# Clamp and square of the first block's activation: from two GpSimd instructions to one VectorE instruction

## The chip, the cores and the metric

The kernel runs on one core of one Trainium2 chip. The metric is device time in microseconds: 1082.85 us is the median of three runs of the kernel before (1081.09 to 1083.65). A core has five queues that run in order and wait for each other by semaphores: TensorE (PE, matrix products into PSUM), VectorE (DVE), ScalarE (ACT), GpSimd (POOL) and SyncE (SP, which issues most transfers).

## The reference

Three parts follow each other. Attention with a soft cap on 4 batches of 12 heads, 448 positions and 64 channels; a feed-forward layer with 768 x 2048 and 2048 x 768 weights; a mixture of 8 experts, each token going to one of them. The change concerns the activation of the feed-forward layer:

```
h = x @ w_in
g = h                      where h >= 1
g = 0                      where h <= -1
g = (h + 1)**2 / 4         between
return g @ w_out
```

The weights w_in and w_out come as 64-bit floats; the kernel takes them as pairs of 32-bit words and converts them itself.

## The kernel before

The 1792 tokens are worked in four blocks b of 448, one for each batch. A block has its attention (six pairs of heads, `attn_gen`), its feed-forward layer (`gemm1` and `gemm2`, together `moe1_gen`) and its routing to the experts (`route_gen`). The feed-forward layer of block b runs woven with the attention of block b + 1. Block 0 is special: beside it the weights are converted from 64 bits (`conv_one`: one ScalarE instruction that writes cv or cvs, three VectorE instructions L1022, L1024 and L1027 on raw or raws, and two transfers for each of 40 pieces, 16 of w_in and 24 of w_out).

`gemm1` makes 16 tiles h (f = 0 to 15) of 128 x 448 in PSUM. All products are made with each operand split in two parts, a rounded one (hi: wh, xh, gh) and its remainder (lo: wl, xl, gl); so each h takes 18 matmuls (L1320 to L1322), nine for each half of its weights. Weights are loaded as wr, rounded to wh by ScalarE (L1289) and their remainder wl made by VectorE (L966). The PSUM tag "m" has two buffers, so h(f + 2) can begin only when h(f) has been read for the last time.

The activation works on a tile g in SBUF. With t = min(relu((h + 1)/2), 1) it is max(h, t * t). In code (`gemm1`): ScalarE makes the relu (L1327); in block 0 (`G_POOL = (0,)`) GpSimd then clamps (L1329) and squares (L1330), while in the blocks 1 to 3 one VectorE instruction does both (L1332); VectorE takes the maximum with h (L1333, the last reading of the PSUM buffer); then ScalarE rounds to gh (L1334) and VectorE makes gl (L966). GpSimd also copies the last keys into a block-diagonal tile kd (L1099) and scales the attention's output x (L1168).

The order on each queue is not that of the code. Every step is declared with `op(engine, cost, ...)`, and `Plan.run` simulates the engines with these costs, in nanoseconds, and issues the steps in the order in which they would become ready; where two are ready, the earlier declared one goes first, shifted by `URGENCY` of its tile. So an engine, a cost or a number of steps that is changed at one place can move others. The costs that matter here are `gs(448)` = 710 for the clamp, `g_(448)` = 1090 for the square and `d1(448)` = 531 for a VectorE instruction. From the last part on (the experts) the order is written out by hand.

Of the kernel before, what the change touches and what calls it, by code (L numbers as in the profile page):

```python
# [15 lines left out]
ALU = mybir.AluOpType  # L16
# [5 lines left out]
B, H, S, D = 4, 12, 448, 64  # L22
# [17 lines left out]
PACE = 65000  # L40

URGENCY = {'h': 30, 'slot': 38, 'ev': -60, 'kq': -15, 'gh': 60, 't': 16, 'w': -8, 'yr': -15, 'sc': 8, 'rt': 16, 'yt': 15, 'lt': -38, 'lp': 60, 'pt': 15, 'ph': -22, 'kd': 45, 'xh': -45, 'g': -60, 'den': 22, 'pick': -60, 'vn': 60, 'fill': -60}
G_POOL = (0,)


def constants():
# [645 lines left out]
class Plan:  # L692
# [13 lines left out]
    def op(self, eng, cost, fn, rd=(), wr=(), dma=0, more=(), duty=1.0, lazy=None):  # L706

        s = Step()
        s.eng, s.cost, s.fn, s.dma, s.more, s.duty = eng, cost, fn, dma, more, duty
        s.lazy = self.BACKLOG if lazy is None else lazy  # L710
        s.users, s.gates = [], []
        s.name = str(getattr(wr[0][0], "name", wr[0]))
        s.rank = (len(self.steps) + URGENCY.get(re.search("[a-z]+", s.name)[0], 0), len(self.steps))
        deps = set()
        syms = set()
        rd = list(rd) + [(x[0].gate, 0) for x in (*rd, *wr) if isinstance(x[0], Sym) and x[0].gate]
        for k in rd:
            if k in self.last:
                deps.add(self.last[k])
            self.reads.setdefault(k, []).append(s)  # L720
        for k in wr:
            if k in self.last:
                deps.add(self.last[k])
            deps.update(self.reads.pop(k, ()))
            self.last[k] = s
        for k in (*rd, *wr):
            if isinstance(k[0], Sym):
                syms.add(k[0])
                if k[0].within:
                    syms.add(k[0].within[0])  # L730
        deps.discard(s)
        s.deps = len(deps)
        for d in deps:
            d.users.append(s)
        s.syms = sorted(syms, key=lambda x: x.name)
        for x in s.syms:
            if x.left == 0:
                self.order.setdefault((x.tag, x.name if x.tag is None else None), []).append(x)
            x.left += 1
        s.ready = 0.0  # L740
        self.steps.append(s)
# [166 lines left out]
def kernel(ctx, tc, q, k, v, cap, w_in, w_out, w_gate, w1, w2, consts, cols, out):  # L908

    nc = tc.nc  # L910
    PE, ACT, DVE, POOL, SP = nc.tensor, nc.scalar, nc.vector, nc.gpsimd, nc.sync
# [37 lines left out]
    op = P.op  # L949
# [7 lines left out]
    d1 = lambda n: 1.04 * n + 65  # L957
    d2 = lambda n: 0.52 * n + 70
    g_ = lambda n: 2.3 * n + 60
    gs = lambda n: 1.45 * n + 60  # L960
    mm = lambda n, N=S: n * N / 2.37
    KDC = 210
    SPQ, PQ = 560, 1040
# [1 line left out]
    def sub_lo(eng, out, a, hi):  # L965
        eng.tensor_sub(out, a, hi.bitcast(F32))  # L966
# [283 lines left out]
    def split_x(b):  # L1250
        for i in range(NDC):
            x = xs[b, i]
            op("ACT", a_(S), lambda x=x, i=i: ACT.copy(xh[b].t[:, i], x.t), rd=[(x, 0), (x, 1)], wr=[(xh[b], i)])
            op("DVE", d1(S), lambda x=x, i=i: sub_lo(DVE, xl[b].t[:, i], x.t, xh[b].t[:, i]),
               rd=[(x, 0), (x, 1), (xh[b], i)], wr=[(xl[b], i)])
# [5 lines left out]
    def unit_load(u):  # L1261
        b, i = divmod(u, NU)
        if b >= B:
            return
        n = 384 if i < 2 * NFC else 512
        while b == 0 and words and conv_n[0] <= (i // 2 if i < 2 * NFC else i - NFC):
            conv_one(conv_n[0])
        r = Sym(MP, [128, 512], F32, "wr", 3, f"wr{u}")
        if words:
            src = wi_s[i] if i < 2 * NFC else wo_s[i - 2 * NFC]  # L1270
            go = lambda: SP.dma_start(r.t[:, :n], src)
        else:
            if i < 2 * NFC:
                f, hf = divmod(i, 2)
                src = w_in[hf * 384 : hf * 384 + 384, f * 128 : f * 128 + 128]
            else:
                d, g = divmod(i - 2 * NFC, 4)
                src = w_out[g * 512 : g * 512 + 512, d * 128 : d * 128 + 128]
            go = lambda: SP.dma_start(r.t[:, :n].rearrange("p (a f) -> p a f", f=128), src.rearrange("(a p) f -> p a f", p=128))
        op("SP", SPQ, go, rd=[("w", i)], wr=[(r, 0)], dma=n * 512)  # L1280
        wraw[u] = r, n

    def unit_split(u):
        if u >= B * NU:
            return
        r, n = wraw.pop(u)
        hi = Sym(MP, [128, 512], F32R, "wh", 4, f"wh{u}")
        lo = Sym(MP, [128, 512], F32R, "wl", 4, f"wl{u}")
        op("ACT", a_(n), lambda: ACT.copy(hi.t[:, :n], r.t[:, :n]), rd=[(r, 0)], wr=[(hi, 0)])  # L1289
        op("DVE", d1(n), lambda: sub_lo(DVE, lo.t[:, :n], r.t[:, :n], hi.t[:, :n]), rd=[(r, 0), (hi, 0)], wr=[(lo, 0)])  # L1290
        wsp[u] = hi, lo

    def step(u):
        unit_load(u + 4)
        unit_split(u + 2)
# [3 lines left out]
    def gemm1(b):  # L1299
        u = b * NU  # L1300
        if b == 0:
            for i in range(4):
                unit_load(i)
            unit_split(0)
            unit_split(1)
        split_x(b)
        for f in range(NFC):
            if b == B - 1 and f % 2:
                pm = Sym(PSE, [128, 512], F32, "y", 2, f"h{b}_{f}")
            else:  # L1310
                pm = Sym(PM, [128, 512], F32, "m", 2, f"h{b}_{f}")
            for hf in range(2):
                step(u)
                hi, lo = wsp.pop(u)
                u += 1

                def go(hi=hi, lo=lo, hf=hf, pm=pm):
                    for a in range(3):
                        i = 3 * hf + a
                        PE.matmul(pm.t[:, :S], part_of(hi, a), xh[b].t[:, i], start=i == 0, stop=False)  # L1320
                        PE.matmul(pm.t[:, :S], part_of(hi, a), xl[b].t[:, i], start=False, stop=False)  # L1321
                        PE.matmul(pm.t[:, :S], part_of(lo, a), xh[b].t[:, i], start=False, stop=i == NDC - 1)  # L1322

                op("PE", mm(9), go, rd=[(hi, 0), (lo, 0)] + [(x[b], 3 * hf + a) for x in (xh, xl) for a in range(3)], wr=[(pm, 0)])
                yield 1701
            t = Sym(XP, [128, S], F32, "g", 2, f"g{b}_{f}")
            op("ACT", 520, lambda t=t, pm=pm: ACT.activation(t.t, pm.t[:, :S], AF.Relu, bias=half, scale=0.5), rd=[(pm, 0), ("half", 0)], wr=[(t, 0)])  # L1327
            if b in G_POOL:
                op("POOL", gs(S), lambda t=t: POOL.tensor_scalar(out=t.t, in0=t.t, scalar1=1.0, scalar2=None, op0=ALU.min), wr=[(t, 0)])  # L1329
                op("POOL", g_(S), lambda t=t: POOL.tensor_mul(t.t, t.t, t.t), wr=[(t, 0)])  # L1330
            else:
                op("DVE", d1(S), lambda t=t: DVE.scalar_tensor_tensor(out=t.t, in0=t.t, scalar=1.0, in1=t.t, op0=ALU.min, op1=ALU.mult), wr=[(t, 0)])  # L1332
            op("DVE", d1(S), lambda t=t, pm=pm: DVE.tensor_max(t.t, pm.t[:, :S], t.t), rd=[(pm, 0)], wr=[(t, 0)])  # L1333
            op("ACT", a_(S), lambda t=t, f=f: ACT.copy(gh[b].t[:, f], t.t), rd=[(t, 0)], wr=[(gh[b], f)])  # L1334
            op("DVE", d1(S), lambda t=t, f=f: sub_lo(DVE, gl[b].t[:, f], t.t, gh[b].t[:, f]), rd=[(t, 0), (gh[b], f)], wr=[(gl[b], f)])
# [29 lines left out]
    def moe1_gen(b):  # L1365
        yield from gemm1(b)
        yield from gemm2(b)
# [157 lines left out]
    b = B - 1  # L1525
    P.gate("opened", lambda: opened(0), (AP, PA))
    weave((gemm1(b), 56000), (chosen(), 50000))

    def swap():
# [81 lines left out]
    with tc.manual_schedule(engines=set(engines)):  # L1611
        b = B - 1
# [64 lines left out]
```

## Time and profile before

| | |
|---|---|
| runs of the kernel before | 1083.65, 1081.09, 1082.85 us |
| profiled execution | 1089.11 us, its span 1087.3 us |
| TensorE busy (matmul) | 1020.2 us, 94% of the span |
| VectorE busy | 527.8 us, 49% |
| ScalarE busy | 527.7 us, 49% |
| GpSimd busy | 176.7 us, 16% |
| mean granted TensorE clock | 0.977 of full speed |

A row of the profile gives an engine, a line of the code, the tile written and the tiles read. "Busy" counts an instruction from its start to its end; a TensorE that waits for an operand or for a free PSUM buffer is idle, and the profile names what ended that idle time. The granted clock is told as a share of full speed (2.4 GHz); 0.50 is the lower of the two levels, 1.2 GHz.

### The profile page before, as it was taken

The page shows a single profiled execution, that of the slowest core. Times are in us where ns is not written, and L with a number is a line of the kernel's source. Part 1 is how long each engine was busy: PE and PEld are TensorE (multiplying, and loading weights), DVE is VectorE, ACT ScalarE, POOL GpSimd, SP SyncE. Part 2 cuts the span into 40 slices and gives each one's busy share as a digit, 9 for nine tenths or more (in the row PEclk, how much of TensorE's full clock was granted, in tenths as well). Part 3 has the DMA queues.
Part 4 walks back from the last instruction along what each step waited for, and adds up shares of the span by engine and source line. Part 5 has one row for each costly group of instructions (what it writes and reads, how often), then busy time and mean ns, then how long its engine had stood idle before and what let it go on. Part 6 is the DMA issues. An engine that isn't in the chain of part 4 may idle for free. (4 is left out here: it accounts for less than half of the span.)

```text
span 1087.3 us, 17434 instructions
## 1 busy us (share of the span) xinstructions
PE 1020.2 (94%) x5546; PEld 784.8 (72%) x5546; DVE 527.8 (49%) x1038; ACT 527.7 (49%) x872; POOL 176.7 (16%) x231
## 2 busy tenths in 40 slices
PE   5887799899999999999999999999999999999995
PEld 2434676678776776966776789889767768889994
DVE  5786799776556653356664237663460101111110
ACT  4876577564656755376666345463332212222221
POOL 1123465310031100011001001100311111111110
PEclk9998899999999999999999999999999999999998
DMA  7777877879454444344443335683128884211111
GB/s 212 222 208 214 252 215 222 254 220 286 141 100 121 111 115 107 107 114 99 109 115 88 97 96 120 206 270 105 41 59 310 309 296 164 61 47 46 45 45 34
DMA packets 167810, 162.57 MB, mean 150 GB/s; under 512 B 90805, under 2 KB 139437, under 8 KB 167682
## 3 DMA queue, kind: packets, MB, share of 16 engines
q1 hardware_dynamic: 164274, 148.06, 46.8%
q0 software_dynamic: 3408, 13.00, 3.6%
q8 instruction: 56, 0.92, 0.3%
q14 instruction: 72, 0.59, 0.2%
HBM read 190.39 MB, written 24.39 MB: 198 GB/s over the span
## 5 line engine op out<-in xcount | busy, mean ns | idle before, releaser
L966 DVE TENSOR_TENSOR wl<-wr,wh 128x384 fp32r<-128x384 f32 (+1 forms) x224 | 143.1, 640 | 134.1 <-ACT wh L1289 133.3
L1289 ACT CAST wh<-wr 128x384 fp32r<-128x384 f32 (+1 forms) x224 | 124.2, 556 | 126.5 <-PE y L1353 69.9
L1320 PE MATMUL h<-xh,wh 128*128 128x448 f32 x384 | 150.0, 391 | 12.1 <-DVE g L1333 11.7
L1322 PE MATMUL h<-xh,wl 128*128 128x448 f32 x384 | 144.0, 375 | 2.0 <-DVE wl L966 2.0
L1352 PE MATMUL y<-gh,wh 128*128 128x448 f32 x384 | 144.0, 375 | 0.4 <-DVE g L1333 0.4
L1321 PE MATMUL h<-xl,wh 128*128 128x448 f32 x384 | 144.2, 376 | 0.0
L1354 PE MATMUL y<-gh,wl 128*128 128x448 f32 x384 | 140.8, 367 | 0.9 <-DVE wl L966 0.9
L1353 PE MATMUL y<-gl,wh 128*128 128x448 f32 x384 | 140.5, 366 | 0.0
L1320 PEld LDWEIGHTS h<-xh,wh 128*128 128x128 f32 x384 | 74.6, 194 | 49.5 <-issue 23.2
L1135 PE MATMUL pv<-t,vn 128*64 128x448 f32 x384 | 96.9, 587 | 11.0 <-ACT t L1115 3.8
L1114 ACT ACTIVATE t<-sc,csc 128x896 f32<-128x896 f32 x96 | 87.2, 914 | 25.1 <-PE sc L1105 15.0
L500 DVE TENSOR_TENSOR hl<-ht,hh 128x512 fp32r<-128x512 f32 x26 | 18.0, 691 | 164.9 <-ACTq L599 159.9
L1115 ACT ACTIVATE t<-t,capx 128x896 f32<-128x896 f32 x96 | 91.0, 951 | 2.1
L1352 PEld LDWEIGHTS y<-gh,wh 128*128 128x128 f32 x384 | 72.1, 188 | 22.4 <-issue 15.3
L1322 PEld LDWEIGHTS h<-xh,wl 128*128 128x128 f32 x384 | 74.7, 195 | 9.1 <-DVE wl L966 2.4
L1321 PEld LDWEIGHTS h<-xl,wh 128*128 128x128 f32 x384 | 74.8, 195 | 5.9 <-DVE xl L966 0.2
L1354 PEld LDWEIGHTS y<-gh,wl 128*128 128x128 f32 x384 | 72.1, 188 | 7.9 <-DVE wl L966 1.9
L512 PE MATMUL ey<-w2h,hh 128*128 128x384 f32 x208 | 75.3, 362 | 2.7 <-issue 2.7
L1353 PEld LDWEIGHTS y<-gl,wh 128*128 128x128 f32 x384 | 72.2, 188 | 5.5
L514 PE MATMUL ey<-w2h,hl 128*128 128x384 f32 x208 | 70.6, 339 | 0.0
L513 PE MATMUL ey<-w2l,hh 128*128 128x384 f32 x208 | 70.5, 339 | 0.0
L480 PE MATMUL ph<-w1h,ex 128*128 128x512 f32 x156 | 64.3, 412 | 2.1 <-issue 2.1
(254 smaller groups left out, 1637.7 us busy)
## 6 DMA issues: line engine op xcount, KB each, us to landing
s<-in_moe_w_dram SPq DMA_DIRECT2D x84, 512.0 KB
s<-in_moe_w_dram SPq DMA_DIRECT2D x104, 384.0 KB
wr<-wi_s SPq DMA_DIRECT2D x128, 192.0 KB
wr<-wo_s SPq DMA_DIRECT2D x96, 256.0 KB
raws<-in_moe_w_in_dram SPq DMA_DIRECT2D x12, 768.0 KB
raw<-in_moe_w_out_dram SPq DMA_DIRECT2D x12, 512.0 KB
wo_s<-cv SPq DMA_DIRECT2D x24, 256.0 KB
kq<-in_k_dram SPq DMA_DIRECT2D x48, 112.0 KB
```

Source lines behind the costliest of these rows:

```text
L512: nc.tensor.matmul(o, hh[:, i], self.w2h[f][:, c], start=f == 0, stop=False)
L966: eng.tensor_sub(out, a, hi.bitcast(F32))
L1114: op("ACT", a_(n * S) + 35, lambda: ACT.activation(t.t[:, :n], pt.t[:, :n, :S], AF.Tanh, scale=csc), rd=[(pt, 0), ("cap", 0)], wr=all_)
L1115: op("ACT", a_(n * S) + 85, lambda: ACT.activation(t.t[:, :n], t.t[:, :n], AF.Exp, scale=capx), wr=all_)
L1135: PE.matmul(pvs.t[rows(j), :S], s["vn"][:, c, j], px(j), start=c == 0, stop=c == 3)
L1289: op("ACT", a_(n), lambda: ACT.copy(hi.t[:, :n], r.t[:, :n]), rd=[(r, 0)], wr=[(hi, 0)])
L1320: PE.matmul(pm.t[:, :S], part_of(hi, a), xh[b].t[:, i], start=i == 0, stop=False)
L1321: PE.matmul(pm.t[:, :S], part_of(hi, a), xl[b].t[:, i], start=False, stop=False)
L1322: PE.matmul(pm.t[:, :S], part_of(lo, a), xh[b].t[:, i], start=False, stop=i == NDC - 1)
L1352: PE.matmul(pm.t[:, :S], part_of(hi, f % 4), gh[b].t[:, f], start=f == 0, stop=False)
L1353: PE.matmul(pm.t[:, :S], part_of(hi, f % 4), gl[b].t[:, f], start=False, stop=False)
L1354: PE.matmul(pm.t[:, :S], part_of(lo, f % 4), gh[b].t[:, f], start=False, stop=f == NFC - 1)
```

## The change

In block 0 the clamp and the square become the VectorE instruction of the other blocks: (t min 1) * t. The constant `G_POOL` and the cost `gs` go. The lines behind them move up by two to six.

```diff
-G_POOL = (0,)
...
-    gs = lambda n: 1.45 * n + 60
...
-            if b in G_POOL:
-                op("POOL", gs(S), lambda t=t: POOL.tensor_scalar(out=t.t, in0=t.t, scalar1=1.0, scalar2=None, op0=ALU.min), wr=[(t, 0)])
-                op("POOL", g_(S), lambda t=t: POOL.tensor_mul(t.t, t.t, t.t), wr=[(t, 0)])
-            else:
-                op("DVE", d1(S), lambda t=t: DVE.scalar_tensor_tensor(out=t.t, in0=t.t, scalar=1.0, in1=t.t, op0=ALU.min, op1=ALU.mult), wr=[(t, 0)])
+            op("DVE", d1(S), lambda t=t: DVE.scalar_tensor_tensor(out=t.t, in0=t.t, scalar=1.0, in1=t.t, op0=ALU.min, op1=ALU.mult), wr=[(t, 0)])
```

Since the planner sees other engines and costs, the order of other steps moves too. GpSimd loses the 32 instructions, VectorE gains 16; of some 5500 TensorE rows about 50 stand elsewhere, nearly all in blocks 0 and 1. Three places matter.

VectorE around the first two activations, before. The names carry the pair's or tile's number f and a serial number; wl is a weight remainder, raws and cvs belong to the conversion, kl is a remainder of the keys:

```order
L1027 SCALAR_TENSOR_TENSOR cvs<-cvs,raws 128x768
L966 TENSOR_TENSOR wl_1178<-wr_1096,wh_1174 128x384
L1333 TENSOR_TENSOR g_0_1172<-h_0_968,g_0_1172 128x448
L1022 TENSOR_SCALAR raws<-raws 128x768
L966 TENSOR_TENSOR wl_1217<-wr_1142,wh_1201 128x384
L1024 SCALAR_TENSOR_TENSOR raws<-raws 128x768
L966 TENSOR_TENSOR kl_1228<-pt_0_1184,kh_1215 128x448
L1333 TENSOR_TENSOR g_1_1199<-h_1_1012,g_1_1199 128x448
```

And VectorE at the same place now:

```order
L1025 SCALAR_TENSOR_TENSOR cvs<-cvs,raws 128x768
L1326 SCALAR_TENSOR_TENSOR g_0_1172<-g_0_1172 128x448
L964 TENSOR_TENSOR wl_1178<-wr_1096,wh_1174 128x384
L1327 TENSOR_TENSOR g_0_1172<-h_0_968,g_0_1172 128x448
L1020 TENSOR_SCALAR raws<-raws 128x768
L1326 SCALAR_TENSOR_TENSOR g_1_1201<-g_1_1201 128x448
L1022 SCALAR_TENSOR_TENSOR raws<-raws 128x768
L1327 TENSOR_TENSOR g_1_1201<-h_1_1012,g_1_1201 128x448
```

The new instruction (now L1326) stands two places ahead of the maximum (now L1327), with a wl or a conversion between; kl has moved to a later place.

TensorE between h3 and h4, before (sc are attention scores, pt transposed keys or queries, pv and su the products with values and ones):

```order
L1322 MATMUL h_3_1247<-xh_624,wl_1217 128x448
L1080 MATMUL pt_1_1290<-ct,kq_1106 128x112 x4
L1105 MATMUL sc_3_1296<-qh_1043,kd 128x448 x2
L1105 MATMUL sc_3_1296<-ql_1061,kd 128x448
L1135 MATMUL pv_1123<-t_2_1219,vn_98 64x448 x2
L1135 MATMUL pv_1123<-t_3_1312,vn_98 64x448 x2
L1139 MATMUL su_1337<-ta_1134,one 32x448
L1139 MATMUL su_1337<-t_3_1312,one 32x448
L1139 MATMUL su_1337<-ta_1134,one 32x448
L1139 MATMUL su_1337<-t_3_1312,one 32x448
L1320 MATMUL h_4_1356<-xh_624,wh_1241 128x448
```

TensorE between h3 and h4 now:

```order
L1320 MATMUL h_3_1228<-xh_624,wl_1238 128x448
L1106 MATMUL sc_2_1274<-qh_1043,kh_1004 128x448 x2
L1106 MATMUL sc_2_1274<-qh_1043,kl_1010 128x448 x2
L1106 MATMUL sc_2_1274<-ql_1061,kh_1004 128x448 x2
L1078 MATMUL pt_1_1292<-ct,kq_1106 128x112 x4
L1318 MATMUL h_4_1317<-xh_624,wh_1223 128x448
```

The group sc_2, which stood in front of h2, has come here; sc_3 now follows h4, one pv follows h5, and the other pv and su follow h6. On ScalarE the relus of g2 and g3 stood behind a tanh of sc_3; they now stand behind the tanh of sc_2 and one wh.

VectorE for the activations of h2 and h3, before (rt are sums of the attention, qh rounded queries):

```order
L966 TENSOR_TENSOR wl_1326<-wr_1265,wh_1306 128x384
L1024 SCALAR_TENSOR_TENSOR raw_1189<-raw_1189 128x768
L1162 TENSOR_TENSOR rt_1288<-rt_1288 32x2x14
L1085 CAST qh_1344<-pt_1_1290 128x448
L1027 SCALAR_TENSOR_TENSOR cv_1271<-cv_1271,raw_1189 128x768
L1333 TENSOR_TENSOR g_2_1320<-h_2_1205,g_2_1320 128x448
L1163 RECIPROCAL rt_1288<-rt_1288 32x2x14
L1333 TENSOR_TENSOR g_3_1323<-h_3_1247,g_3_1323 128x448
```

And VectorE for the same activations now:

```order
L964 TENSOR_TENSOR wl_1300<-wr_1250,wh_1290 128x384
L1326 SCALAR_TENSOR_TENSOR g_2_1298<-g_2_1298 128x448
L1326 SCALAR_TENSOR_TENSOR g_3_1302<-g_3_1302 128x448
L1327 TENSOR_TENSOR g_2_1298<-h_2_1191,g_2_1298 128x448
L1327 TENSOR_TENSOR g_3_1302<-h_3_1228,g_3_1302 128x448
L1025 SCALAR_TENSOR_TENSOR cv_1265<-cv_1265,raw_1189 128x768
L964 TENSOR_TENSOR gl_1288<-g_2_1298,gh_1245 128x448
L964 TENSOR_TENSOR gl_1288<-g_3_1302,gh_1245 128x448
L964 TENSOR_TENSOR wl_1338<-wr_1263,wh_1307 128x384
L1160 TENSOR_TENSOR rt_1271<-rt_1271 32x2x14
L964 TENSOR_TENSOR kl_1350<-pt_0_1184,kh_1207 128x448
```

Four activation instructions now stand together, and kl, from which GpSimd makes the copies kd that sc_3 reads, stands behind them.

## Rows read from the trace of the kernel before

**Rows 1.** Windows of all engines: stretch, then busy us (instructions); PEclk, DMA share, GB/s

```profile
100.00:210.00 110.00, 94.60 (x453) 70.12 (x449) 91.61 (x138) 67.83 (x111) 56.09 (x50) 0.93 0.79 235
210.00:300.00 90.00, 89.12 (x471) 66.56 (x469) 59.18 (x106) 54.36 (x90) 7.84 (x15) 1.00 0.74 226
```

**Rows 2.** Waits of TensorE, 95 to 215 us: us in total, times, longest

```profile
PE h L1320 <- DVE g L1333: 11.7, 6, 4.7
```

**Rows 3.** Groups by line, GpSimd, 100 to 212 us: busy us, mean ns | idle before

```profile
L1329 POOL TENSOR_SCALAR g<-g 128x448 f32<-128x448 f32 x16 | 26.4, 1650 | 42.4 <-ACT g L1327 42.3
L1330 POOL TENSOR_TENSOR g<-g 128x448 f32<-128x448 f32 x16 | 16.8, 1052 | 1.0
```

**Rows 4.** Groups by line and shape, ScalarE, 100 to 212 us

```profile
L1289 ACT CAST wh<-wr 128x384 fp32r<-128x384 f32 x26 | 13.1, 505 | 4.7 <-PE h L1321 2.6 <-PE h L1322 1.2 <-DMA wr<-wi_s 0.9
...
L1114 ACT ACTIVATE t<-sc,csc 128x896 f32<-128x896 f32 x10 | 10.1, 1009 | 0.9 <-PE sc L1108 0.8
L1327 ACT ACTIVATE g<-h,half 128x448 f32<-128x448 f32 x16 | 10.0, 630 | 3.8 <-PE h L1322 3.8
```

**Rows 5.** Groups by line and shape, VectorE, 100 to 212 us

```profile
L966 DVE TENSOR_TENSOR wl<-wr,wh 128x384 fp32r<-128x384 f32 x26 | 18.2, 700 | 2.8 <-ACT wh L1289 2.8
...
L1027 DVE SCALAR_TENSOR_TENSOR cv<-cv,raw 128x512 int32<-128x512 int32 x11 | 10.2, 931 | 0.0
L1333 DVE TENSOR_TENSOR g<-h,g 128x448 f32<-128x448 f32 x16 | 9.8, 616 | 8.2 <-POOL g L1330 8.2
L1024 DVE SCALAR_TENSOR_TENSOR raw<-raw 128x512 int32<-128x512 int32 x11 | 9.6, 876 | 0.3
```

**Rows 6.** The same, VectorE, 212 to 330 us

```profile
L966 DVE TENSOR_TENSOR wl<-wr,wh 128x384 fp32r<-128x384 f32 x16 | 8.9, 555 | 10.5 <-ACT wh L1289 10.5
...
L1024 DVE SCALAR_TENSOR_TENSOR xraws_xh<-xraws_xh 128x512 int32<-128x512 int32 x6 | 4.2, 692 | 0.1
L1027 DVE SCALAR_TENSOR_TENSOR cv<-cv,xraws_xh 128x512 int32<-128x512 int32 x6 | 4.1, 690 | 0.1
...
L1332 DVE SCALAR_TENSOR_TENSOR g<-g 128x448 f32<-128x448 f32 x6 | 3.7, 622 | 7.1 <-ACT g L1327 7.1
L1333 DVE TENSOR_TENSOR g<-h,g 128x448 f32<-128x448 f32 x6 | 3.7, 617 | 0.0
```

**Rows 7.** Timeline of all engines around h2: start us, us, engine, line [idle before]

```profile
105.16 1.37 DVE L1024 SCALAR_TENSOR_TENSOR raws<-raws 128x768 int32<-128x768 int32 x1
...
105.93 0.47 PE L1108 MATMUL sc<-qh,kh 64*128 64x448 f32 x2
...
107.44 1.28 DVE L966 TENSOR_TENSOR wl<-wr,wh 128x384 fp32r<-128x384 f32 x1
...
108.65 0.61 DVE L1333 TENSOR_TENSOR g<-h,g 128x448 f32<-128x448 f32 x1
...
109.31 0.52 PE L1320 MATMUL h<-xh,wh 128*128 128x448 f32 x1 [2.52 <-DVE g L1333]
```

**Rows 8.** Windows of 1 us, TensorE: busy us (instructions), PEclk, DMA share, GB/s

```profile
112.00:113.00 1.00, 1.00 (x5) 0.50 1.06 358
...
133.00:134.00 1.00, 1.00 (x5) 0.75 0.73 171
```

**Rows 9.** Timeline of TensorE around h4

```profile
118.59 0.65 PE L1105 MATMUL sc<-qh,kd 128*128 128x448 f32 x2
...
121.77 0.97 PE L1135 MATMUL pv<-t,vn 128*64 128x448 f32 x4 [1.43 <-ACT t L1115]
...
128.31 0.74 PE L1320 MATMUL h<-xh,wh 128*128 128x448 f32 x1 [4.67 <-DVE g L1333]
```

**Rows 10.** Timeline of GpSimd around h4

```profile
119.58 2.89 POOL L1099 CAST kd<-kh 64x64 fp32r<-64x64 f32 x2 [6.54 <-PE sc L1105]
...
126.66 1.82 POOL L1330 TENSOR_TENSOR g<-g 128x448 f32<-128x448 f32 x2
```

**Rows 11.** Timeline of TensorE near the end of the first product

```profile
201.18 0.47 PE L1320 MATMUL h<-xh,wh 128*128 128x448 f32 x1 [2.67 <-DVE g L1333]
```

## The prediction

> **What bounds the kernel now.** I began with the windows by stage. Behind 210 us TensorE is the bound: it is busy 89.12 of 90 us at full clock [rows 1], so whatever is saved ahead of 210 us can reach the end, and nothing behind it waits for the instructions that the diff touches. The first block's first product lies in 100 to 210 us. There TensorE is busy only 94.60 of 110 us and its mean granted clock is 0.93, while VectorE is busy 91.61 and GpSimd 56.09 us [rows 1].
>
> Then I read who holds TensorE there: 11.7 us in 6 waits for L1333, the maximum that frees the PSUM buffer of an h [rows 2]. Two such buffers exist, so h2 cannot begin before the maximum on h0. Last, the chain that leads to L1333. Today it is relu 0.63 us (ScalarE), clamp 1.65 and square 1.05 (GpSimd), maximum 0.62 (VectorE): 3.95 us without queueing [rows 3 to 5].
>
> **What is removed and added.** GpSimd loses 16 clamps and 16 squares: 26.4 + 16.8 = 43.2 us [rows 3]. Nothing else gains from its free time, since GpSimd is nowhere the bound. VectorE gains 16 of the L1332 form that blocks 1 to 3 already run, at 0.622 us each [rows 6]. Back to back, an instruction begins a little before its predecessor ends (wl began at 107.44 and lasted 1.28, the next began at 108.65: 0.07 us [rows 7]; I reckon with 0.09), so the load is about 16 x 0.53 = 8.5 us.
>
> What VectorE gets back: in 100 to 212 us several of its forms are longer than behind it. The weight remainder wl takes 0.700 against 0.555 us (26 of them: 3.8 us), cv 0.931 against 0.690 (11: 2.7), raw 0.876 against 0.692 (11: 2.0) [rows 5, 6]. That is 8.5 us. The maximum, with one operand in PSUM, is not longer (0.616 against 0.617). GpSimd's busy time is the difference of the two stretches, and 43.2 of its 56.09 us go, so I credit three quarters: 6.5 us. The bounds are 0 (another cause) and 8.5. VectorE's load then changes by 8.5 - 6.5 = +2 us, between 0 and +8.5; its 8.2 us of waiting for GpSimd [rows 5] cover that.
>
> The Trainium skill (SBUF — State Buffer, section "SBUF: two separate sides") says that GpSimd shares a port pair with VectorE, exclusively and for a whole instruction, when the VectorE instruction has two SBUF inputs. The longer wl and the unchanged maximum [rows 5, 6] agree with it; that the mean grows by only 0.15 us, far less than a clamp lasts, shows that most instructions meet no GpSimd one. The rule also speaks against the change: the new instruction has two SBUF inputs and can be held by what GpSimd keeps, the kd and x work, 56.09 - 43.2 = 12.9 of 110 us [rows 1, 3]. At one hit in seven and 0.7 us each this would be 16 x 0.14 x 0.7 = 1.6 us by the rule (an estimate), and the sum below would be 4 instead of 5.5 us.
>
> The chain becomes relu 0.63, new instruction 0.62, mostly one wl of 0.55 that the planner puts between, and maximum 0.62: 2.4 us against 3.95, so 1.5 us shorter [rows 4 to 6]. What that is worth I read at three places.
>
> **Place A, h2.** TensorE stops at 106.79 and begins h2 at 109.31 [rows 7]. In the new order the VectorE queue is raws (begins 105.16, now unstretched, next after 0.87), cvs (0.87), the new instruction (0.53), wl (0.47), maximum: it begins at about 107.9, not 108.65. So h2 begins 0.75 us earlier. But the planner, which reckons on an earlier buffer, has moved the group sc_2 behind h3; those 0.86 us (105.93 to 106.79) were work inside the wait. Net -0.1 us: nothing. The clock, at 0.50 after this wait [rows 8], drops as before.
>
> **Place B, h4.** Here the trace has its longest wait. Work resumes with pt and sc_3 (118.59) and TensorE then waits 1.43 and 4.67 us until h4 begins at 128.31 [rows 9]. GpSimd first does four kd casts, 119.58 to about 124.0, and ends the two squares at 128.48 [rows 10]. Now, with h3 done at about 118.3 - 0.75 = 117.5: sc_2 to 118.4 and its latency, tanh 1.0 (from 118.8), wh 0.5, two relus (pitch 0.53, the second ends at 121.3), new instruction on g3 to 121.9, maximum on g2 to 122.5, h4 at about 122.6. That is 5.7 us earlier. Not yet done then are sc_3, the two pv and su: 128.31 - 4.67 - 118.59 - 1.43 = 3.6 us of work that today stands inside the wait. Net +2.1 us. Bounds: -3.6 if h4 still begins at 128.3, and +5.7 if all the deferred work finds a later wait to hide in. The clock ran at half from 128.31 until late in 133 to 134 [rows 8], costing about 2.6 us; the new wait of some 4 us (with pt inside) is still longer than the one at A, so I take it that the clock drops again, for the shorter time seen at A, and credit 0.8 (bounds 0 and 2.6).
>
> **Place C, h6 to h15.** Of the 11.7 us, 11.7 - 2.52 - 4.67 - 2.67 = 1.8 us are three short waits [rows 2, 7, 9, 11], each under 0.9; a chain 1.5 us shorter removes them. The wait of 2.67 before 201.18 [rows 11] shrinks by 1.5, and the dip of the clock behind it with it (about 1.7 us by the same kind of reckoning; I take half, 0.9). Sum +4.2; bounds 0 and 6.2.
>
> **New waits.** At B the cast kl moves from ahead of the first maxima to behind gl of g3, and sc_3 needs GpSimd's copies of it; VectorE reaches kl near 126 and h4 covers TensorE until about 127.7, so 0 to 1 us is late there. Other moved groups (one sc, one pv between h and y; in block 1 a few rows around its route) have no wait today that I can price. I charge 1.5 us for all, with bounds 0 and 6.
>
> **Sum.** -0.1 + 2.1 + 0.8 + 4.2 - 1.5 = 5.5 us. The profiled execution took 1089.11 us (its span of 1087.3 and 1.8 around it), so it would take 1083.6. The median of the three runs is 1082.85, 6.3 below the profiled one; the waits are those of an order that is the same in both, so I subtract the same 5.5 us: **1077.3 us**.
>
> **Rivals.**
> 1. The gain is whole: all 11.7 us of waits go and about 3 of the dips, 14.7 us, giving 1068. For it: VectorE's load hardly grows. Against it: the reordering uses up places A and B in part, and relu on g2 now stands behind the tanh of a group that itself waits for h3.
> 2. It is given back to the transfers: the DMA share is 0.79 in this stretch and 0.74 in the next [rows 1], and 1.06 in single microseconds [rows 8]. The w_out conversions follow on the heels of their use; if data cannot come earlier, the y product waits and the time stays at about 1082.5. Against it: 5.5 us fewer over 200 us lift the share by 3% only.
> 3. Slower, at place B: the filler of 3.6 us was moved away from the wait, but the wait stays, because tanh, wh, two relus and four VectorE instructions stand in series after h3, and any one late (a weight transfer, a conversion in front) moves h4. It decides at h4 later than 128.31 - 3.6 = 124.7; I reckon 122.6, a margin of 2.1 us. At today's 128.3 the price is 3.6 us: 1086.5.
> That the change does not do what it says is excluded by the new order: no such GpSimd instruction is left, and 16 VectorE ones stand in.
>
> **How the numbers follow.** Forecast 53%, rival 1 15%, rival 2 15%, rival 3 17%. A measurement of this kernel tells about 0.2% (2.2 us) from no change. The forecast's own range, 1073 to 1080, is on the faster side, as is rival 1: faster 68%. Rival 2 is no change, 15%, and rival 3 slower, 17%. The range reaches down to 1068, the full gain, and up to 1085, where a good half of rival 3 lies above.
>
> **What would show it.** In 95 to 215 us the waits for the maximum should fall from 11.7 to about 5 us, nearly all of it at A and B; VectorE's busy time there should stay within 90 to 95 us although 16 instructions more run, with wl at 0.56 to 0.60 us; h4 should begin 5 to 6 us earlier; block 1 should begin earlier by the whole gain. I am wrong if wl stays at 0.70, if h4 begins later than 124.7, or if waits for VectorE's wl, kl or ql take the place of those for the maximum.

## The result, and the profile after

The changed kernel takes 1068.26 us (1066.93 to 1072.70, four runs) against 1082.88 us of the kernel before in the same session: ratio 0.9868, 95% interval 0.9830 to 0.9906. Run once more in a later session (e9 below) it stood at 0.9896 (0.9858 to 0.9934). I use the mean of the two, 0.9882 +- 0.0027, or 12.8 us of 1085, when it is compared with experiments of other sessions. The direction was forecast and the size was not: 5.5 us forecast, 14.6 us in the first comparison and 12.8 us over both.

The profiled execution of the changed kernel took 1066.93 us (span 1065.1, granted clock 0.985). These windows of all engines answer to [rows 1]:

```profile
100.00:210.00 110.00, 104.41 (x531) 78.65 (x530) 93.76 (x164) 76.18 (x122) 16.96 (x22) 0.98 0.87 269
210.00:300.00 90.00, 88.06 (x466) 65.59 (x465) 62.27 (x121) 55.39 (x94) 7.00 (x12) 0.98 0.65 195
```

In the 110 us of the first product TensorE is busy 104.41 instead of 94.60 us, at a clock of 0.98 instead of 0.93. GpSimd falls from 56.09 to 16.96 us. VectorE rises by only 2.15 us in the same window, although it does 16 instructions more and its other work there has advanced too. The waits of TensorE in 95 to 215 us, against [rows 2]:

```profile
PE h L1318 <- DVE g L1327: 4.5, 2, 2.9
PE pv L1133 <- ACT ev L1152: 3.4, 1, 3.4
PE pt L1078 <- ACT t L1112: 1.1, 1, 1.1
```

The maximum (now L1327) is waited for 4.5 us in two pieces instead of 11.7 us in six. Both pieces stand before 119 us, at the places A and B of the prediction; from there to 215 us no wait of a quarter of a microsecond is left. (The wait for ev lies ahead of the first rectifier, the ScalarE instruction that writes g0, and is there in both kernels.) TensorE's timeline shows the three waits over a quarter of a microsecond that are left behind the first rectifier:

```profile
105.68 0.47 PE L1318 MATMUL h<-xh,wh 128*128 128x448 f32 x1 [1.60 <-DVE g L1327]
...
115.16 0.60 PE L1078 MATMUL pt<-ct,kq 112*128 112x112 f32 x4 [1.10 <-ACT t L1112]
...
118.66 0.74 PE L1318 MATMUL h<-xh,wh 128*128 128x448 f32 x1 [2.90 <-DVE g L1327]
```

h2 begins at 105.68 (before 109.31 [rows 7]) and h4 at 118.66 (before 128.31 [rows 9]). The windows of 1 us, against [rows 8] (the third number from the right is the granted clock):

```profile
106.00:107.00 1.00, 1.00 (x6) 0.93 (x5) 0.36 (x1) 1.00 (x2) 0.00 (x0) 1.00 1.11 361
...
120.00:121.00 1.00, 1.00 (x4) 0.91 (x3) 1.00 (x4) 0.48 (x1) 0.00 (x0) 0.50 1.18 273
121.00:122.00 1.00, 1.00 (x5) 0.88 (x5) 1.00 (x4) 0.53 (x2) 0.00 (x0) 0.70 1.23 331
```

Behind A it no longer falls (1.00 from 105 to 118 us, where the kernel before had 0.50 behind h2); behind B it is back in the window from 121 us, having run TensorE at half speed for 3 us instead of 5.2. VectorE by line and shape, 100 to 205 us, against [rows 5, 6]:

```profile
L964 DVE TENSOR_TENSOR wl<-wr,wh 128x384 fp32r<-128x384 f32 x26 | 15.2, 589 | 1.1 <-ACT wh L1287 1.1
L1326 DVE SCALAR_TENSOR_TENSOR g<-g 128x448 f32<-128x448 f32 x16 | 9.8, 620 | 1.3 <-ACT g L1325 1.2
L1327 DVE TENSOR_TENSOR g<-h,g 128x448 f32<-128x448 f32 x16 | 9.8, 619 | 0.0
```

wl is down from 0.700 to 0.589 us, the new instruction takes the 0.62 us that it takes in the other blocks, and VectorE no longer waits for GpSimd ahead of the maximum (8.2 us before).

Where the profiles part: the first copy of a finished y tile, which ends the stage, starts 17.4 us earlier.

```profile
202.43 0.53 ACT L1357 COPY yt<-y 128x448 f32<-128x448 f32 x1 [0.99 <-PE y L1348]
```

Before it was this one:

```profile
219.80 0.53 ACT L1363 COPY yt<-y 128x448 f32<-128x448 f32 x1 [0.99 <-PE y L1354]
```

Of the 17.4 us, 2.5 were there at the first rectifier already, ahead of anything that the change touches, and are chance. By the last y copy of block 0 the lead is 13.6 us, since the changed kernel now waits for a w_out weight, and the granted clock falls to 0.50 behind that wait until 261.5 us (1.6 us):

```profile
257.25 0.47 PE L1346 MATMUL y<-gh,wh 128*128 128x448 f32 x1 [1.55 <-ACT wh L1287]
258.26 0.74 PE L1348 MATMUL y<-gh,wl 128*128 128x448 f32 x1 [0.34 <-DVE wl L964]
```

In block 1 it gains 5 us again, where the kernel before had waits of 0.53 and 1.16 us near 326 us, with a dip of the clock behind them (1.7 us), and the changed one has none. e1 below, in the old order, has none either, so this gain isn't the order's. At the end the profiles differ by 22.2 us, but the profiled execution of before was 6.2 us above its median.

### The profile page after: what moved, and what is told of

It is laid out like the page before. It is cut to its first block, busy times and chain, and to the rows that moved or that the text cites. A ratio compares the mean times of both kernels' runs of the same rounds, so it can differ in the third digit from the quotient of the medians.

```text
span 1065.1 us, 17407 instructions
## 1 busy us (share of the span) xinstructions
PE 1010.5 (95%) x5546; PEld 778.8 (73%) x5546; DVE 526.9 (49%) x1054; ACT 527.5 (50%) x872; POOL 135.0 (13%) x199
## 5 line engine op out<-in xcount | busy, mean ns | idle before, releaser
L1318 PE MATMUL h<-xh,wh 128*128 128x448 f32 x384 | 146.9, 383 | 4.8 <-DVE g L1327 4.5
L1320 PE MATMUL h<-xh,wl 128*128 128x448 f32 x384 | 141.8, 369 | 1.4 <-DVE wl L964 1.4
L1319 PE MATMUL h<-xl,wh 128*128 128x448 f32 x384 | 141.4, 368 | 0.0
L1112 ACT ACTIVATE t<-sc,csc 128x896 f32<-128x896 f32 x96 | 87.4, 916 | 30.5 <-PE sc L1103 16.1
L1325 ACT ACTIVATE g<-h,half 128x448 f32<-128x448 f32 x64 | 40.5, 635 | 49.6 <-PE h L1320 48.1
```

What stands on the lines that cost most here:

```text
L1112: op("ACT", a_(n * S) + 35, lambda: ACT.activation(t.t[:, :n], pt.t[:, :n, :S], AF.Tanh, scale=csc), rd=[(pt, 0), ("cap", 0)], wr=all_)
```

## The experiments

Three theories. "port": GpSimd's big instructions lengthen VectorE's, and VectorE is nearly full in this stage, so taking them away is the gain. "chain": what counts is that the buffer of h comes free sooner. "order": the planner's new order is worth something by itself. A kernel's time is given as a ratio to the kernel before on the same chip, with its 95% interval; 0.001 is 1.1 us.

For the stage alone I also read, in each profile, the time from the second rectifier's start to the first y copy. It is one execution each, so it locates a difference rather than proving it. The wait at A lies ahead of the second rectifier; from the first, with A inside, the stretch is 115.4 us before, 100.5 in the changed kernel (102.4 in e9), 103.9 in e1, 114.0 in e2, 107.2 in e12 and 106.9 in e13.

| kernel | ratio to before | interval | stage, us |
|---|---|---|---|
| before | 1 | | 110.1 |
| changed kernel | 0.9868 | 0.9830 to 0.9906 | 95.9 |
| e1 new instruction, old order | 0.9923 | 0.9890 to 0.9955 | 98.6 |
| e2 new order, GpSimd's instructions | 0.9975 | 0.9947 to 1.0003 | 108.8 |
| e3 changed, with GpSimd load | 0.9958 | 0.9932 to 0.9984 | 105.5 |
| e4 e1, with GpSimd load | 0.9990 | 0.9966 to 1.0015 | 109.6 |
| e5 changed, GpSimd load that only writes | 0.9883 | 0.9848 to 0.9917 | 100.1 |
| e7 changed, with VectorE load | 0.9921 | 0.9894 to 0.9947 | 99.5 |
| e8 changed, scaling x on VectorE | 0.9884 | 0.9843 to 0.9925 | 98.3 |
| e9 changed, again | 0.9896 | 0.9858 to 0.9934 | 95.8 |
| e10 loads of e5 and e7 together | 0.9942 | 0.9915 to 0.9968 | 102.3 |
| e11 changed, longer chain | 0.9908 | 0.9875 to 0.9941 | 99.1 |
| e12 before, GpSimd reads almost nothing | 0.9965 | 0.9938 to 0.9991 | 101.6 |
| e13 before, no clamp and square | 0.9900 | 0.9868 to 0.9931 | 101.9 |

**Two by two: order and instruction.** e1 keeps before's order on every queue; the clamp's step issues nothing and the square's step issues the new VectorE instruction:

```diff
-                op("POOL", gs(S), lambda t=t: POOL.tensor_scalar(...), wr=[(t, 0)])
-                op("POOL", g_(S), lambda t=t: POOL.tensor_mul(t.t, t.t, t.t), wr=[(t, 0)])
+                op("POOL", gs(S), lambda: None, wr=[(t, 0)])
+                op("POOL", g_(S), lambda t=t: DVE.scalar_tensor_tensor(...), wr=[(t, 0)])
```

> The order of all queues is that of the kernel before; only the two GpSimd instructions are replaced, at the place of the square, by the one on VectorE. Theory 'chain' (the gain is the shorter way from relu to maximum): -10 to -13 us against before, 1070 to 1073. Theory 'port' (the gain is that GpSimd no longer holds VectorE up): the same here. Theory 'order' (the planner's new order brings the gain, here above all in block 1, where the two profiles differ by 5 us): only -4 to -7, 1076 to 1079, with block 1's wait for ql still there.

Measured 1076.67 us, 0.9923: 8.4 us faster than before without the new order. That is less than the 10 to 13 us on record for "chain" and "port", and the time lies in the range of "order"; but the wait for ql in block 1, which "order" wanted to see, is gone. The waits of TensorE from 95 to 215 us in e1 show how much goes without the new order:

```profile
PE h L1320 <- DVE g L1333: 5.5, 3, 2.1
PE pv L1135 <- ACT t L1115: 1.6, 2, 1.4
PE sc L1108 <- DVE ql L966: 0.3, 1, 0.3
```

Of the short waits of the old kernel only the 0.3 us for ql is left.

e2 is the reverse: the changed kernel's order, with GpSimd's clamp and square issued where the new instruction stands.

```diff
...
+                if b == 0:
+                    POOL.tensor_scalar(out=t.t, in0=t.t, scalar1=1.0, scalar2=None, op0=ALU.min)
+                    POOL.tensor_mul(t.t, t.t, t.t)
+                else:
+                    DVE.scalar_tensor_tensor(...)
...
```

> The order of all queues is that of the changed kernel, but clamp and square of block 0 run on GpSimd, issued at the place of the new instruction. 'Chain' and 'port': no gain in block 0, 0 to +3 us there; with the 5 us that the profiles show in block 1, 1078 to 1086. 'Order': -6 us or more, 1077 or less.

Measured 1084.36 us, 0.9975: no worse than before, perhaps 2.7 us better, although in this order VectorE stands still 18.8 us for GpSimd ahead of its maxima. From the other side, the changed kernel against e1, the order is worth 0.0041 +- 0.0043, or 4.4 us. Neither alone excludes zero; both exclude that the moved groups cost several microseconds. The profiles show no gain of the order either: from the first rectifier to the first y copy of block 1 the changed kernel is 16.1 us shorter than before, in e9 13.7, and e1 15.4.

**GpSimd's load put back off the chain.** e3 is the changed kernel, and e4 is e1, with a clamp and a square of the same size on GpSimd behind each rounding, from gh into a spare tile whose content nobody waits for:

```diff
+                if b == 0:
+                    POOL.tensor_scalar(out=spare, in0=gh[b].t[:, f].bitcast(F32), scalar1=1.0, scalar2=None, op0=ALU.min)
+                    POOL.tensor_mul(spare, spare, spare)
```

> The changed kernel, and GpSimd does one clamp and one square for each of the 16 tiles on a spare tile, reading gh; nobody waits for the result. 'Chain': 1068 to 1071, since the way from relu to maximum stays short. 'Port': VectorE's wl, cv and raw are longer again by about 8 us in sum, GpSimd's kd and x are late, and half of the gain is gone: 1074 to 1079.

> As e1_instr_old_order, and the same 32 idle instructions on GpSimd. 'Chain': within 2 us of e1. 'Port': 5 us or more above e1.

Measured e3 1080.82 us (0.9958) and e4 1084.78 us (0.9990). The load costs 0.0076 +- 0.0037 (8.2 us) in the new order and 0.0067 +- 0.0041 (7.3 us) in the old one, though nothing of the computation waits for its result: most of what the change gains. e3 lies above even the range on record for "port" (1074 to 1079), e4 inside its own (5 us or more above e1). VectorE by line and shape in e3, 100 to 205 us:

```profile
L965 DVE TENSOR_TENSOR wl<-wr,wh 128x384 fp32r<-128x384 f32 x26 | 18.1, 700 | 0.6 <-ACT wh L1288 0.6
L965 DVE TENSOR_TENSOR gl<-g,gh 128x448 fp32r<-128x448 f32 x15 | 11.6, 781 | 0.6 <-ACT gh L1330 0.6
...
L1023 DVE SCALAR_TENSOR_TENSOR raw<-raw 128x512 int32<-128x512 int32 x10 | 8.8, 878 | 0.0
...
L1328 DVE TENSOR_TENSOR g<-h,g 128x448 f32<-128x448 f32 x16 | 9.7, 609 | 0.0
```

wl is at before's 0.700 us again, raw at 0.878 (before 0.876), and the maximum, which reads PSUM, stays at 0.61. So GpSimd's work causes the stretch that the prediction had read out of [rows 5, 6]; with gl (0.620 in the changed kernel) and the smaller forms it comes to some 10 us of VectorE time.

**Is it the reading, the queue, or plain VectorE time?** e5 keeps GpSimd as busy but lets it write only; e7 adds VectorE time and leaves GpSimd alone; e10 does both.

```diff
# e5, behind each rounding of block 0
+                    POOL.tensor_copy(spare[:, :8], gh[b].t[:, f, :8].bitcast(F32))
+                    for _ in range(6):
+                        POOL.memset(spare, 0.0)
# e7, behind each maximum of block 0
+                    DVE.tensor_max(spare, t.t, t.t)
```

> The changed kernel, and behind each of block 0's 16 roundings GpSimd copies 8 columns of it to a spare tile and then fills the 128x448 spare tile with zeros six times: GpSimd is kept busy as in e3, but reads almost nothing from SBUF, it only writes. Theory 'port' (GpSimd's reads of SBUF stretch VectorE's copies): VectorE's wl copy between 100 and 205 us stays at 0.58 to 0.61 us and the time at 1066 to 1071. Theory 'queue' (what costs is that kd and x of the attention stand behind other work in GpSimd's queue): about e3's time, 1079 to 1083, with waits of VectorE and TensorE for kd and x, wl near 0.60. Rival, any GpSimd work (also writing) stretches VectorE: wl 0.65 to 0.72 and 1078 to 1083.

> The changed kernel with one more VectorE maximum of 128x448 into a spare tile behind each maximum of block 0: 16 x 0.53 to 0.62 = 8.5 to 9.9 us of plain VectorE work, in VectorE's order, nothing on GpSimd. Theory 'port' as I now hold it (a stretch of VectorE costs what VectorE time costs there, as VectorE is the bound between 100 and 205 us): 1075 to 1081, near e3's time, VectorE 100 to 102 busy of 110 us, clock 0.93 to 0.95. Theory 'covered' (as my sum had it, most VectorE time lies beside TensorE work): 1069 to 1073, and then e3's loss isn't the stretch of VectorE but something else of GpSimd's load.

> The changed kernel with both loads together: one more VectorE maximum of 128x448 into a spare tile behind each maximum of block 0 (10.3 us, as in e7), and GpSimd kept busy by writing zeros (56 us, as in e5), in after's order. e3, where GpSimd's load reads and so stretches VectorE by about 8.4 us, stood at 0.9958 of before. Theory 'sum' (e3's loss is the lost VectorE time plus a busy GpSimd queue): 0.994 to 0.997 of before, 1078 to 1082, waits near 152 and 180 us as in e3. Theory 'read' (GpSimd's reading costs more than the VectorE time it takes): 0.990 to 0.993, as e7 alone, 1074 to 1078.

e5: 1072.01 us, a microsecond above the range of "port"; by its ratio, 0.9883, level with the changed kernel (+- 0.0044, so some microseconds for the busy queue aren't excluded; the stage of its profile is 4.2 us longer). GpSimd is busy 71.33 of 110 us as in e3 (71.14). VectorE there:

```profile
L965 DVE TENSOR_TENSOR wl<-wr,wh 128x384 fp32r<-128x384 f32 x26 | 14.5, 560 | 0.9 <-ACT wh L1288 0.9
...
L1021 DVE TENSOR_SCALAR raw<-raw 128x512 int32<-128x512 int32 x10 | 5.9, 586 | 6.1 <-ACT cv L1020 6.1
```

wl is at 0.560, as short as behind the stage in the old kernel (0.555 [rows 6]). The stretch of the forms with two operands in SBUF needs a GpSimd instruction that reads; the form with one operand is longer (0.586 against 0.430 us in the changed kernel) beside one that only writes, as it was beside the old kernel's clamps and squares (0.601). The Trainium skill (SBUF — State Buffer, section "SBUF: two separate sides") draws this line for two-input instructions: they meet GpSimd at the shared port only when GpSimd reads. These rows agree.

e7: 1075.31 us, 0.9921, so 10.3 us of maxima cost 0.0039 +- 0.0038, 4.2 us; VectorE's window shows it full:

```profile
100.00:210.00 110.00, 102.15 (x500) 75.74 (x501) 103.11 (x180) 72.79 (x119) 17.50 (x22) 0.95 0.83 257
```

The time touches the range on record for "port", but the changed kernel beside it (e9) was above its own; by ratio the loss lies between "covered" (nothing lost) and "port" (all of it): about four tenths, with an error as large. e10: 1077.69 us, 0.9942; the ratio is inside the range of "sum", the time 0.3 us inside that of "read". It is 0.0060 +- 0.0038 behind the changed kernel, near e3's 0.0076. VectorE time and a busy GpSimd queue together thus explain e3 within the error; whether reading costs still more can't be told from these runs.

**The chain.** e11 lengthens it in the changed kernel by two tiny GpSimd copies between the rectifier and the new instruction:

```diff
+                if b == 0:
+                    POOL.tensor_copy(t.t[:, :8], t.t[:, :8])
+                    POOL.tensor_copy(t.t[:, :8], t.t[:, :8])
```

> The changed kernel, but between the rectifier and VectorE's clamp and square GpSimd copies 8 columns of the tile onto themselves twice (block 0): the chain from the rectifier to the maximum is longer by 1.2 to 1.6 us, about as long as before the change, while GpSimd reads almost nothing and VectorE does the same work; VectorE, in order, also waits. Theory 'chain' (the shorter chain is the main gain): 1080 to 1084. Theory 'port' (the GpSimd's load going is the main gain, some 8 to 10 us, the chain 0 to 4): 1071 to 1076, wl near 0.58 us, and PE's waits for the maximum 4.5 -> 7 to 9 us.

Measured 1074.62 us, 0.9908, 2.8 us behind the changed kernel (+- 4.6). The copies took 0.36 and 0.25 us, so the chain grew by some 0.6 us and not by the 1.2 to 1.6 that I wanted; TensorE waited 7.0 us for the maximum instead of 4.5. The time is in the range of "port"; on the chain it shows the sign of the waits, no more, and it can't exclude that the chain costs several microseconds.

e12 and e13 take before's own order. In e12 GpSimd's clamp becomes a copy of 8 columns onto themselves and three fills of a spare tile, its square such a copy; in e13 both steps issue nothing. Both kernels leave the clamp and the square out, so VectorE's maximum works on other values.

```diff
# e12
+    def small(t, n):
+        POOL.tensor_copy(t.t[:, :8], t.t[:, :8])
+        for _ in range(n):
+            POOL.memset(spare, 0.0)
...
+                op("POOL", gs(S), lambda t=t: small(t, 3), wr=[(t, 0)])
+                op("POOL", g_(S), lambda t=t: small(t, 0), wr=[(t, 0)])
```

> The kernel before with its own order, but GpSimd's clamp is a copy of 8 columns onto themselves and three fills of a spare tile, and its square such a copy: the chain stays about as long (2.6 us on GpSimd instead of 2.7), GpSimd is as long busy, VectorE gets no more work, and GpSimd reads almost nothing; the clamp and the square themselves are left out. Theory 'port': wl 0.700 -> 0.56 to 0.59 us, VectorE's busy time down by 6 to 9 us, and 1075 to 1081 (0.991 to 0.996 of before). Theory 'chain' (and the sum of the prediction, which gave 6.5 us of the stretch back at no price): 1081 to 1085.

> The kernel before with its own order, without block 0's 16 clamps and squares: neither GpSimd nor VectorE does them (they are left out), so VectorE's maximum follows the rectifier. Against e12 (0.9965) the chain loses GpSimd's 2.6 us and GpSimd's queue; against e1 (0.9923) 16 VectorE instructions of 0.62 us are missing. Theory 'chain' (GpSimd's place in the chain costs more than its stretch, and VectorE's 16 instructions cost about what e7's extra load did, 3 to 4 us): 0.986 to 0.991, 1070 to 1076. Rival 'covered' (the 16 VectorE instructions cost nothing, so e1 has the whole gain of this order): 0.991 to 0.995, 1076 to 1080.

e12: 1079.75 us, in the range of "port"; 0.9965. With GpSimd still in the chain but hardly reading, 3.8 us (1.0 to 6.7) come back; wl is 0.585. This isn't the reading alone: the substitutes keep GpSimd for 2.1 us a tile and the clamp and square for 2.7, so the chain is shorter too. e13: 1072.66 us, 0.9900, in the range of "chain"; with GpSimd out of the chain another 0.0065 +- 0.0041, 7.1 us, is gained. The profiles don't show this step: from the first rectifier to the first y copy e12 and e13 take 107.2 and 106.9 us, and either is some 8 us shorter than before. e13 waits less (9.8 us against 12.1 in waits over 0.15 us) but loses more to the clock (3.3 us against 1.6). How the gain divides between GpSimd's reading and its place in the chain therefore stays open; that the two together are worth some 11 us is what e13 against before shows.

What the place in the queue does can be seen at B. This is GpSimd in e12:

```profile
118.00 3.53 POOL L1106 CAST kd<-kh 64x64 fp32r<-64x64 f32 x2 [6.25 <-PE sc L1112]
121.59 1.46 POOL L1106 CAST kd<-kl 64x64 fp32r<-64x64 f32 x2
123.11 0.19 POOL L949 COPY g<-g 128x8 f32<-128x8 f32 x1
```

and TensorE behind it:

```profile
127.22 0.74 PE L1327 MATMUL h<-xh,wh 128*128 128x448 f32 x1 [5.16 <-DVE g L1340]
```

The rectifiers of g2 and g3 were done by 119.6, but GpSimd takes instructions in order, and the kd casts keep it until 123.1: the longest wait of the old kernel, where the casts end near 124.0 [rows 10], is mostly a wait behind casts in GpSimd's queue. In e13, with GpSimd out of the chain, the longest wait at A and B is 1.85 us.

e13 against e1 (0.9923) prices the 16 new VectorE instructions at 0.0023 +- 0.0045: 2.5 us, not told from zero, so "chain" and "covered" aren't settled on this point. Place C in e13 holds a surprise. Neither clamp nor square is left, and TensorE still waits 3.50 us, more than before [rows 11]. ScalarE:

```profile
186.68 0.66 ACT L1021 ACTIVATE cv<-raw 128x512 f32<-128x512 f32 x1 [3.19 <-DMA raw<-in_moe_w_out_dram]
187.24 0.63 ACT L1327 ACTIVATE g<-h,half 128x448 f32<-128x448 f32 x1
```

VectorE:

```profile
189.04 0.68 DVE L1027 SCALAR_TENSOR_TENSOR cv<-cv,raw 128x512 int32<-128x512 int32 x1
189.65 0.61 DVE L1333 TENSOR_TENSOR g<-h,g 128x448 f32<-128x448 f32 x1
```

TensorE:

```profile
190.31 0.74 PE L1320 MATMUL h<-xh,wh 128*128 128x448 f32 x1 [3.50 <-DVE g L1333]
```

The old order puts the rectifier behind a conversion that waits 3.19 us for its w_out piece, and the maximum behind three more VectorE instructions of the conversion. So the wait at C is not the chain's alone. From the rectifier's start to the maximum's end it is 4.3 us before, 3.6 in e1 and 3.0 in e13, while the conversion ahead of the rectifier waits 0.66, 0.76 and 3.19 us for its piece; TensorE waits 2.67, 1.45 and 3.50. The changed kernel has no wait at C.

**A candidate, and the changed kernel again.** e8 moves what else GpSimd does at full size, the scaling x, to VectorE in blocks 0 and 1 (the planner reorders).

```diff
+        if b in (0, 1):
+            op("DVE", d1(S), lambda: DVE.tensor_mul(x.t, ev.t, x.t), rd=[(ev, 0)], wr=[(x, 0), (x, 1)])
+        else:
...
```

> The changed kernel with the attention's scaling x (128x448, two full operands) of blocks 0 and 1 on VectorE instead of GpSimd; the planner lays out the rest again. On GpSimd one x takes 2.03 us beside VectorE between 100 and 205 us. Theory 'port': what is left of the stretch goes (wl 0.589 to 0.56), and x adds about 0.7 us on VectorE each: 1064 to 1069. Rival 'load' (VectorE is so full that each 0.7 us counts): 1069 to 1074.

> The changed kernel once more, beside the other three on the same chip: 1066 to 1071 by every theory, ratio 0.983 to 0.990.

e8: 1070.93 us, 0.9884, in the range of "load" and not told from the changed kernel, although wl falls to 0.551. e9: 1073.95 us, 0.9896, above its expected time, as the kernel before was in that session (1086.11 us); its ratio is inside. Its stage takes 95.8 us as in the first profile, but place A differs:

```profile
105.66 0.74 PE L1318 MATMUL h<-xh,wh 128*128 128x448 f32 x1 [2.28 <-DVE g L1327]
```

This wait is 2.28 us, and from 106 to 109 the granted clock is 0.50. After 1.60 us it was 1.00 throughout. The buffer did not come free sooner in the first profile. VectorE's maximum stands there at

```profile
105.01 0.62 DVE L1327 TENSOR_TENSOR g<-h,g 128x448 f32<-128x448 f32 x1
```

and in e9 at

```profile
104.99 0.62 DVE L1327 TENSOR_TENSOR g<-h,g 128x448 f32<-128x448 f32 x1
```

TensorE came to it 0.7 us later in the first profile, since the clock was at 0.50 until past 101 us there (an earlier dip, behind the wait for ev) and at 1.00 from 99 us in e9. The shorter wait at A is chance. Nor does the length of the wait alone tell what the clock does: at the same place it stayed at 1.00 behind 1.98 us in e11 and fell to 0.50 behind 1.94 us in e1.

## Why the prediction was right in sign and short in size

The terms of its sum, beside what the profiles of the changed kernel and of e1 (the new instruction in the old order) gain over the kernel before in the stage:

| term | forecast, us | changed, us | e1, us | from (changed kernel) |
|---|---|---|---|---|
| A, wait | -0.1 | +0.9 | +0.6 | 2.52 to 1.60 |
| A, clock | 0 | +1.7 | 0 | 3.4 us of TensorE work at half clock (109.6 to 113.0) before, none after |
| B, waits | +2.1 | +2.1 | +2.5 | 1.43 + 4.67 to 1.10 + 2.90 |
| B, clock | +0.8 | +1.1 | +0.9 | 5.2 to 3.0 us at half clock |
| C, waits | +3.3 | +4.5 | +3.1 | 1.8 + 2.67 to none |
| C, clock | +0.9 | +1.7 | +1.7 | 0.83 of 200 to 210 to 1.00 |
| new waits | -1.5 | +2.2 | +1.9 | short waits for rt, wh, y, qh and ql gone, none added |
| sum | 5.5 | 14.2 | 10.7 | first rectifier to first y copy: 14.8 and 11.5 shorter |

The step that failed is the term for new waits. I took the moved groups as a loss of 1.5 us, for which no row gave a price, and left the short waits for rt, wh, y, qh and ql (2.2 us in the kernel before) at nothing. The profiles show no new wait and the short ones gone: 3.7 of the 8.7 us that are missing. It is the instruction that removes them and not the groups that moved, since e1, in the old order, keeps only 0.3 us of them. The order by itself doesn't slow the kernel (e2); with the new instruction the changed kernel is 3.4 us ahead of e1 in the stage, 1.5 in e9's execution. That the order gains is not shown: 2.7 and 4.4 us by the two comparisons of times, each within its error. Place B, the boldest piece of that working, came out at +2.1 as forecast, but e1 has +2.5 there without any group moved.

The second largest shortfall is the clock: 4.5 us measured, 1.7 credited, and 1.7 of it is luck. I let the dip at A stand because the wait there seemed to stay near 2.5 us. In e9, where TensorE comes to A at full clock, the wait is 2.28 us and the dip is there, as forecast; in the first profile an earlier dip had delayed TensorE.

The VectorE term (+8.5 - 6.5, nothing on the path) was right in busy time: 93.76 us, inside the 90 to 95 named, wl inside 0.56 to 0.60. More came back than its three forms: gl went from 0.708 to 0.620 us and the one-operand form on raw from 0.601 to 0.430. The price of nothing is doubtful. e7 puts VectorE time in this stage at about four tenths of itself (0.0039 +- 0.0038), by which the stretch given back and the new load would each be worth 3 to 4 us and nearly cancel; that would be why the sum didn't suffer. The cause of the stretch, GpSimd, is shown by e3 and e5.

At C the forecast held for the old order, +3.1 in e1 against +3.3, though not by the chain alone: the chain went from 4.3 to 3.6 us and not by 1.5, and e13 shows a wait of 3.50 there with no clamp in the chain, behind a conversion that waits for its transfer.

That the time lies in the range on record, 1068 to 1085, is luck in part: 1068.26 is inside by 0.3 us. The forecast's own 1073 to 1080 holds the 1073.95 of e9's session and not the first comparison.

Of the rivals, the first (1068, the whole gain) gave the time, and its two parts are there: 7.2 of the 11.7 us of waits, and more of the clock than its 3 us. The second seems to appear in small: the DMA share rose from 0.79 to 0.87, the y product waited 1.55 and 0.34 us near 257 us, and 3.8 us of the stage's lead were given back there. But e1, as early in the old order (a lead of 15.0 us at the first y copy), gave nothing back, and e2, early by only 3.6 us, gave back 2.9: this loss goes with the new order and not with data that can't come earlier. The third did not happen: h4 began at 118.66, far from its deciding point of 124.7.

In runs the path from before to the changed kernel reads: before to e12 3.8 us, e12 to e13 7.1, e13 to e1 -2.5 (16 VectorE instructions), e1 to the changed kernel 4.4; together 12.8, as such a chain must give. Shown is the whole of the instruction (e1, 8.4 us) and of GpSimd's leaving (e13, some 11 us). The last two steps are within their error, and the split at e12 is open, as said there. Putting GpSimd's load back off the chain costs 8.2 us, which holds the stretch and the queue that kd and x then meet.

## What to carry to other kernels

When work leaves GpSimd beside a nearly full VectorE, ask for three gains: the stretch of VectorE's SBUF forms, the duration in the chain, and the place in GpSimd's queue, where a clamp that is ready can stand behind casts. The runs here show each of them in the rows, and not how the microseconds divide among them. Don't charge each moved group as a loss: price the instruction in the old order first and the order by itself; here most of the gain was the instruction's. And don't book a dip of the clock from the length of one wait: here 1.94 us had one and 1.98 us had none.

## What the runs showed of the hardware that was not expected

- GpSimd's zero fills (56 us of load with the copies) left VectorE's two-operand SBUF form alone (wl 0.560 us in e5) but lengthened the one-operand form on 128x512 from 0.430 to 0.586 us.
- The granted clock held at 1.00 behind waits of 1.60 us (changed kernel) and 1.98 us (e11) at h2 and fell to 0.50 behind 1.94 us (e1) and 2.28 us (e9) at the same place.
- A GpSimd copy of 8 columns took 0.19 us at its shortest and 0.25 to 0.59 us in the means of e5, e10, e11 and e12; a fill of 128x448 took 0.47 to 0.49 us, a clamp of the same tile beside VectorE 1.65 us (before) to 1.94 us (e3).
